# Four attention layers on one core: the last step of the row maxima goes from VectorE to GpSimd, with another table of slots and PSUM banks

## The chip, the core and the metric

One core of a Trainium2 chip runs the whole program. Its engines are TensorE (PE; its weight loads are shown apart as PEld), VectorE (DVE), ScalarE (ACT), GpSimd (POOL) and the DMA queues, issued here by SyncE (SP). Each engine takes its own instructions in order, and engines wait for one another by semaphores. The metric is the device time of one execution in microseconds (us); the median of the runs counts.

## The reference

Four attention blocks on one sequence of S = 2048 rows, D = 576, H = 32 heads of 18 columns, all in float32. Layers 0 and 2 (kind A) have keys and values for each head; layers 1 and 3 (kind B) share one key and one value head.

```python
x = x + A(layernorm(x));  x = x + B(layernorm(x));  x = x + A(layernorm(x));  x = x + B(layernorm(x))

def A(x, wqkv, wo):                        # B: the same with one k and one v for all heads
    q, k, v = split_heads(x @ wqkv)        # [H, S, 18]
    scores = einsum("hqd,hkd->hqk", q, k) * 18 ** -0.5
    p = softmax(scores, axis=-1)
    return merge_heads(einsum("hqk,hkd->hqd", p, v)) @ wo
```

## The kernel before

**Stages.** Each layer has a prologue (layer norm, transposition, projections to q, k and v through HBM), a main part (the attention), and an output projection that runs into the next layer's prologue. The main part works on pairs of heads `p` (16 pairs) and blocks `u` of 512 queries (4 a pair), so it has 64 windows `w = 4p + u` a layer and 256 in the program.

**One window.** The softmax needs the maximum of each query's scores before the exponentials, so every window does two things side by side: it takes the maxima of window `w + 2` (scores with queries on partitions, then a maximum along the row) and the exponentials of window `w` (scores again, now with keys on partitions and with the maximum subtracted inside the product), and multiplies the exponentials by the values. Heads `a = 0, 1` of the pair stand in the two halves of the array and their products run side by side.

**The table of slots.** `UNIT` writes the order of a window by hand. It has 32 slots; each slot is a pair of products, one for each head, and names what reads them: `e` an exponential (ACT), `m` a maximum over 512 keys (DVE, `reduce_max`), `d` a Relu of a score difference (ACT), `t` the combination of that difference with the second product (DVE, one custom instruction and a read of its accumulator). A pair `d`, `t` takes the maximum over two blocks of keys with one DVE instruction. `ee*` and `mm*` let one instruction read both banks. A number behind a slot says how many columns of probabilities-times-values (`oacc`, `pv_cols`) PE does there; 4096 a window. Slots between two numbers are called a group here: PE does the group's products into banks and then the columns.

**The table of banks.** `BANKS` names the two PSUM banks (of seven) that a slot's products go to. Before, it has four rows of 32 slots, used in turn by window. A product waits until the bank's last reader, on ACT or DVE, is done.

**The last step of the maxima.** The 32 partial maxima of a window (8 groups of 4) are columns of `mxd[w % 2]`. When the last is issued, `max_final` makes the negated maximum `neg` [128 x 8] of each group of four with one DVE reduction; GpSimd splits it into a rounded part and a rest (`hl`). Some slots later (`max_store`, `NM_AT = 3` steps) DVE transposes `hl` to `tr`; a DMA stores it, and another (`max_rows`) loads it into the rows of `big` that the exponentials of two windows later read.

**Other names.** `track_banks` wraps PE, ACT and DVE: it replaces the dependencies that come of the one big PSUM tile by waits on the readers of a bank alone (`met` adds what was made by instructions that the call's other operands overlap). `ptile` hands out halves of two-bank SBUF buffers from one list (`halves`), for staging in the prologue. All PE, ACT and DVE work is recorded at line 153, which is the wrapper's; GpSimd's work has its own lines (323 is `copy`).

Of the kernel before, what the change touches and what calls it, by code (L numbers as in the profile page):

```python
# [19 lines left out]
P = 128  # L20
# [44 lines left out]

UNIT = """ee* mt 256 ee* em te 384 md ee* mt 512 me em em 384 me em me 384 ee* me em 448 me mm ee 320
          md em 256 ee* dm mm 384 ee* em me 384 mm* ee em 384 me"""

BANKS = """01 63 45 26 01 36 45 20 13 62 45 03 16 24 01 53
# [6 lines left out]
           46 01 25 36 40 13 56 20 41 56 30 42 01 56 34 25"""  # L78
LAST = "ee* ee* 640 " + "ee* ee* 512 " * 6 + "ee* ee* 384"
LAG = 1152  # L80

# [78 lines left out]
def track_banks(tc, banks):  # L160

    nc = tc.nc
    readers, made = {}, {}

    def span(x):
        row = x.ap[0][0]
        c0 = x.offset % row
        return c0, c0 + sum((n - 1) * step for step, n in list(x.ap)[1:]) + 1

    def others(args):  # L170
        return [x for x in args if isinstance(x, bass.AP) and x.tensor.name != banks.tensor.name]

    def banks_in(args):
        got = set()
        for x in args:
            if isinstance(x, bass.AP) and x.tensor.name == banks.tensor.name:
                c0, c1 = span(x)
                got.update(range(c0 // 512, (c1 - 1) // 512 + 1))
        return got

    def met(args):
        keep = []
        for x in others(args):
            c0, c1 = span(x)
            keep += [i for d0, d1, i in made.get(x.tensor.name, []) if c0 < d1 and d0 < c1]
        return keep

    def free(i, engines, keep):
        for e in engines:
            tc.declare_no_dep(i.ins, group=e, keep=[x.ins for x in keep], reason="other banks")  # L190

    def order(i, earlier):
        for x in earlier:
            tc.add_manual_dep(i.ins, x.ins.name, mybir.DependencyInfo(mybir.DependencyClass.Sync,
                                                                     mybir.DependencyReason.ANTI), reason="one bank")

    def wrote(i, args, kw):
        for b in banks_in(args[:1]):
            last = [x for _, x in readers.pop(b, [])]
            free(i, ("act", "dve"), last + met(args[1:3]))  # L200
            order(i, last)

    def read(engine, other, i, args, kw):
        args = [*args, *kw.values()]
        got = banks_in(args)
        if got:
            beside = [x for b in sorted(got) for e, x in readers.get(b, []) if e == other]
            free(i, (other,), beside + met(args))
            order(i, beside)
            tc.add_to_no_dep_group(engine, i.ins)  # L210
            for x in others(args):
                made.setdefault(x.tensor.name, []).append((*span(x), i))
            for b in got:
                readers.setdefault(b, []).append((engine, i))

    return (Engine(nc.tensor, wrote), Engine(nc.scalar, functools.partial(read, "act", "dve")),
            Engine(nc.vector, functools.partial(read, "dve", "act")))


@with_exitstack  # L220
def tile_kernel(ctx: ExitStack, tc: tile.TileContext, A_x, A_wqkv, A_wo, B_x, B_wq, B_wk, B_wv, B_wo, out):
# [75 lines left out]
    def etile(name):  # L297
        return turn_of("e", name)

    halves = []  # L300

    def two(name):
        return pool.tile([P, 2, 512], F32, tag="p", bufs=8, name=name)

    def ptile(name, shape=(P, 512), dt=F32):
        if not halves:
            t = two(name)
            halves.extend([t[:, 0], t[:, 1]])
        t = halves.pop(0)
        if dt != F32:  # L310
            t = t.bitcast(dt)
        if len(shape) == 2:
            return t
        return t[:, :shape[1] * shape[2]].rearrange("p (a b) -> p a b", a=shape[1])
# [11 lines left out]
    def load_w(c, dsts, srcs, n, hi, lo, spare):  # L326


        raw = pool.tile([P, 640], F32, tag="xh", bufs=2, name="raw") if spare else ptile("raw")
# [24 lines left out]
    splits = []  # L354

    def finish_loads(n=99):
        while splits and n:
# [183 lines left out]
    for layer in range(4):  # L541
# [11 lines left out]
        def project(T, t, filler=False, half=None, terms=TERMS):  # L553
# [16 lines left out]
            if T < 2 and t in (range(4, 9) if is_a else (4,)):  # L570
                key_diff(T, t, ps, r0, r1)
            if filler:
                raw = ptile("evr")
                act.activation(raw[:n], ps[:n], AF.Copy)
                nc.gpsimd.tensor_tensor(ev[1][:n], raw[:n], ev_f[0][:n], op=OP.subtract)
            else:
                dve.tensor_tensor(ev[1][:n], ps[:n], ev_f[0][:n], op=OP.subtract)
            if not is_a and t == 4:
                vt = ptile("vt")
# [10 lines left out]
        def key_diff(T, t, ps, r0, r1):  # L590

            if T == 0:
                k0s[t] = ptile("k0")
                act.activation(k0s[t][r0:r1], ps[r0:r1], AF.Copy)
                return
            kd, lo, hi = k0s.pop(t), ptile("kl"), ptile("kh", dt=F32R)
# [289 lines left out]
            load_q(0, 512, S)  # L886

        def max_final(p, u):
            neg = pool.tile([P, 8], F32, name="neg")
            dve.tensor_reduce(neg, mxs.pop((p, u)).rearrange("p (b k) -> p b k", k=4), axis=AX.X, op=OP.max,  # L890
                                    negate=True)
            hl = nms[p, u] = hls[(4 * p + u) % 2]
            copy(nc.gpsimd, hl[:, 0:8], neg)
            nc.gpsimd.tensor_tensor(hl[:, 8:16], neg, hl.bitcast(F32)[:, 0:8], op=OP.subtract)
# [147 lines left out]
        kept.extend([etile("psm") for _ in range(weave["left"])])  # L1042
        fill[-1][0](*fill[-1][1])
        assert not weave["left"] and not kept
        side = xtile("side", (P, 9, 512), F32)
        late, n_r, n_p, sided = LAG, [0], [0], {}
        for w in range(4 * NPAIR):
# [67 lines left out]
```

## Time and profile before

| what | value |
|---|---|
| median of 3 runs (lowest, highest) | 5566.91 us (5565.56, 5570.06) |
| the profiled execution's own time | 5563.2 us |
| its span, first to last instruction | 5561.4 us |
| busy: PE, DVE, ACT, POOL | 5530.8, 5008.6, 4712.7, 1072.8 us |
| granted clock of TensorE | 0.999 |
| windows in which `neg` is made from `mxd` | 248 of 256 |

A row of the instruction groups reads: line, engine, operation, out<-in, shapes, count, busy us, mean ns of one. A row of the timeline reads: start us, us, engine, line, operation, names, shapes, how many merged, and in brackets the idle time before it and what ended it. DVE and ACT instructions overlap their neighbours at both ends, so what one costs is the distance from its start to the next one's start, which is less than its duration. A busy PE is not a PE at its peak, since the ends of products are modelled.

### The profile page before, as it was taken

The numbers are of one execution on the slowest core, as the hardware profiler recorded it, in microseconds if no ns is written. First come the engines' busy times: TensorE is split into PE (matmuls) and PEld (weight loads), VectorE is DVE, ScalarE is ACT, GpSimd is POOL, SyncE is SP. The second block draws the span as 40 slices with busy tenths as digits, with TensorE's granted clock in tenths as the row PEclk, the third lists the DMA queues.
The fourth block names the chain that finished last, engine by engine and source line by source line (L and its number), as shares of the span: only waits on it lengthen the run. The fifth ranks groups of instructions, "written<-read, shape, count | busy, mean of one in ns | idle before, by whom it ended". The sixth has DMA issues, their size and how long they took to land. (4 is left out here: it accounts for less than half of the span.)

```text
span 5561.4 us, 159140 instructions
## 1 busy us (share of the span) xinstructions
PE 5530.8 (99%) x63772; PEld 3174.9 (57%) x63772; DVE 5008.6 (90%) x9260; ACT 4712.7 (85%) x8020; POOL 1072.8 (19%) x1731
## 2 busy tenths in 40 slices
PE   9999999999999999999999999999999999999999
PEld 7655555555855555555686555555558555555556
DVE  5799999998699999999647999999977999999995
ACT  3599999999289999999625999999992999999995
POOL 3121111112121111112221211111122211111111
PEclk9999999999999999999999999999999999999999
DMA  7311111111421110101253211111114211110102
GB/s 235 114 48 39 40 38 41 37 38 32 129 64 25 24 25 21 25 21 25 62 198 96 51 39 37 40 37 41 34 39 133 54 24 25 24 25 21 25 14 81
DMA packets 295504, 295.03 MB, mean 53 GB/s; under 512 B 151133, under 2 KB 228189, under 8 KB 285041
## 3 DMA queue, kind: packets, MB, share of 16 engines
q1 hardware_dynamic: 294760, 284.85, 18.5%
q8 instruction: 499, 8.18, 0.6%
q14 instruction: 245, 2.00, 0.1%
HBM read 158.77 MB, written 121.95 MB: 50 GB/s over the span
## 5 line engine op out<-in xcount | busy, mean ns | idle before, releaser
L153 DVE TENSOR_REDUCE mxd<-banks 128x1 f32<-128x512 f32 (+1 forms) x6200 | 3995.4, 703 | 92.2 <-PE banks L153 20.4
L153 ACT ACTIVATE pt<-banks 128x512 f32<-128x512 f32 (+1 forms) x4408 | 2887.5, 716 | 136.2 <-PE banks L153 93.8
L153 PE MATMUL banks<-big 62*128 62x512 f32 (+1 forms) x15640 | 2818.4, 435 | 6.9 <-DVE mx L153 3.2
L153 PEld LDWEIGHTS banks<-big 62*128 62x128 f32 (+1 forms) x15640 | 1551.8, 185 | 1301.9 <-DVE mxd L153 499.4
L153 ACT ACTIVATE side<-banks 128x512 f32<-128x512 f32 (+1 forms) x2916 | 1864.7, 684 | 71.6 <-PE banks L153 53.2
L153 PE MATMUL oacc<-pt,vbuf 128*19 128x256 f32 (+3 forms) x21152 | 1287.9, 336 | 0.0
L153 PEld LDWEIGHTS oacc<-pt,vbuf 128*19 128x19 f32 x21152 | 460.4, 98 | 492.8 <-issue 330.8
L973 POOL TENSOR_TENSOR rl<-lt,mone 128x8 f32<-128x8 f32 x256 | 420.0, 1640 | 1634.5 <-DMA lt<-os 1611.2
L153 PE MATMUL oacc<-side,vbuf 128*19 128x128 f32 (+3 forms) x10400 | 684.3, 335 | 0.2 <-DVE ocv L153 0.2
L153 DVE CUSTOM_DVE_ANT_0 side<-banks,side 128x512 f32<-128x512 f32 x744 | 506.7, 681 | 0.0
L323 POOL TENSOR_SCALAR hl<-neg 128x8 fp32r<-128x8 f32 x256 | 51.7, 202 | 2144.2 <-DVE neg L153 2144.2
L153 PE MATMUL oacc<-pt,vy 128*19 128x128 f32 (+1 forms) x7520 | 436.0, 325 | 0.0
L153 PEld LDWEIGHTS oacc<-side,vbuf 128*19 128x19 f32 x10400 | 229.9, 98 | 238.9 <-issue 158.8
L153 PE MATMUL banks<-kd,big 54*128 54x512 f32 x744 | 344.2, 463 | 0.0
L153 ACT ACTIVATE ev<-banks 128x512 fp32r<-128x512 f32 (+3 forms) x107 | 63.6, 597 | 248.4 <-PE banks L153 144.8
L153 PEld LDWEIGHTS oacc<-pt,vy 128*19 128x19 f32 x7520 | 176.4, 98 | 156.0 <-issue 105.8
L153 PE MATMUL banks<-wsm,ot 128*128 128x288 f32 x1792 | 243.7, 296 | 2.1 <-issue 2.1
L153 PEld LDWEIGHTS banks<-wsm,ot 128*128 128x128 f32 x1792 | 238.4, 188 | 6.4 <-issue 5.2
L153 PE MATMUL oacc<-side,vy 128*19 128x128 f32 (+1 forms) x3680 | 232.8, 325 | 0.0
L153 DVE TENSOR_TENSOR ev<-banks,ev 128x512 fp32r<-128x512 f32 (+3 forms) x77 | 52.8, 690 | 183.6 <-ACT ev L153 144.4
L153 PE MATMUL banks<-xx,big 128*128 128x512 f32 (+1 forms) x784 | 198.4, 402 | 5.0 <-ACT evr L153 2.5
L153 PE MATMUL banks<-yx,big 128*128 128x512 f32 (+2 forms) x812 | 196.4, 395 | 5.1 <-DVE yx L153 3.3
(98 smaller groups left out, 2391.5 us busy)
## 6 DMA issues: line engine op xcount, KB each, us to landing
big<-qk_d SPq DMA_DIRECT2D x180, 432.0 KB
qk_d<-ev SPq DMA_DIRECT2D x73, 512.0 KB
qk_d<-ev SPq DMA_DIRECT2D x114, 256.0 KB
rb<-r_d SPq DMA_DIRECT2D x1024, 18.0 KB
o_d<-os SPq DMA_DIRECT2D x1024, 18.0 KB
lt<-os SPq DMA_DIRECT2D x1024, 1.0 KB
o<-o_d SPq DMA_DIRECT2D x62, 256.0 KB
big<-m_d SPq DMA_DIRECT2D x512, 4.0 KB
```

The lines of the kernel that those rows point to most:

```text
L153: i = f(*args, **kw)
L323: eng.tensor_scalar(dst, src, 1.0, 0.0, op0=OP.mult, op1=OP.add)
L973: nc.gpsimd.tensor_tensor(rl, lts.pop((p, u)), mone, op=OP.pow)
```

## The change

- `max_final` no longer uses DVE. Six GpSimd instructions stand for the one reduction: a maximum is written as the positive part of a difference plus the other value, first for columns 0, 1 against 2, 3 of each group (into the new tile `tree`), then for the two that are left. The split into `hl` follows on GpSimd as before.
- `UNIT` and `BANKS` are replaced. A window still has 32 slots, 26 `m` (two of them joined in one `mm*`), 3 `d`, 3 `t` and 32 `e`, 11 groups and 4096 columns; `ee*` stands 7 times where it stood 6 times. `BANKS` has one row of 32 slots for every window.
- `track_banks` compares operands by their exact runs of columns, where it took one span from the first to the last column, and keeps the last 64 instructions that made or read a tensor.
- `ptile` keeps a list of halves for each first letter of a name, and some names change so that they share one (`evr` becomes `raw`, `k0` becomes `first`, `vt` becomes `t`). The first weight load and the key staging of `t == 4` use `ocv`. The lists are emptied before the main part.

```diff
-UNIT = """ee* mt 256 ee* em te 384 md ee* mt 512 me em em 384 me em me 384 ee* me em 448 me mm ee 320
-          md em 256 ee* dm mm 384 ee* em me 384 mm* ee em 384 me"""
+UNIT = """me md em 320 ee* me et 384 em me me 448 em ee* mm 384 ee* dm mm 384 ee* tm ed 512 em mm* ee
+          256 me me 256 ee* mm me 320 em ee* et 448 me ee* mm 384"""
-BANKS = """01 63 45 26 01 36 45 20 13 62 45 03 16 24 01 53
...
+BANKS = """13 06 45 23 16 04 51 23 64 05 12 34 56 03 12 34
+           56 10 23 45 16 02 31 45 62 01 36 45 12 03 45 62"""
@@ track_banks
-    def span(x):
-        row = x.ap[0][0]
-        c0 = x.offset % row
-        return c0, c0 + sum((n - 1) * step for step, n in list(x.ap)[1:]) + 1
+    def runs(x):
+        row, *dims = [list(d) for d in x.ap]
+        at = [x.offset % row[0]]
+        for step, n in dims[:-1]:
+            at = [c + step * i for c in at for i in range(n)]
+        step, n = dims[-1]
+        return [(c, c + step * (n - 1) + 1) for c in at]
...
-                made.setdefault(x.tensor.name, []).append((*span(x), i))
+                made[x.tensor.name] = [*made.get(x.tensor.name, [])[-63:], (runs(x), i)]
@@ tile_kernel
+    tree = cst.tile([P, 8, 4], F32, name="tree")
...
-        if not halves:
+        left = halves.setdefault(name[0], [])
+        if not left:
             t = two(name)
-            halves.extend([t[:, 0], t[:, 1]])
-        t = halves.pop(0)
+            left.extend([t[:, 0], t[:, 1]])
+        t = left.pop(0)
...
-                k0s[t] = ptile("k0")
+                k0s[t] = ocv if t == 4 else ptile("first")
@@ max_final
+            mx = mxs.pop((p, u)).rearrange("p (b k) -> p b k", k=4)
+            above, left = tree[:, :, 0:2], tree[:, :, 2:4]
+            nc.gpsimd.tensor_tensor(above, mx[:, :, 0:2], mx[:, :, 2:4], op=OP.subtract)
+            nc.gpsimd.tensor_scalar(above, above, 0.0, None, op0=OP.max)
+            nc.gpsimd.tensor_tensor(left, above, mx[:, :, 2:4], op=OP.add)
             neg = pool.tile([P, 8], F32, name="neg")
-            dve.tensor_reduce(neg, mxs.pop((p, u)).rearrange("p (b k) -> p b k", k=4), axis=AX.X, op=OP.max,
-                                    negate=True)
+            nc.gpsimd.tensor_tensor(neg, left[:, :, 0], left[:, :, 1], op=OP.subtract)
+            nc.gpsimd.tensor_scalar(neg, neg, 0.0, -1.0, op0=OP.max, op1=OP.mult)
+            nc.gpsimd.tensor_tensor(neg, neg, left[:, :, 1], op=OP.subtract)
             hl = nms[p, u] = hls[(4 * p + u) % 2]
```

**What moves on DVE.** The rows below are DVE's queue from the end of one window's maxima to a little behind the transposition, in the main part of layer 0, before the change and after it. `ISA` is the custom instruction `t`, the `ISA` row behind it the read of its accumulator; `PE_49`, `DVE_49`, `Pool_49` and the like are the semaphores of the engines, `DMAHW` those of DMAs.

```order
L153 ISA side_1944,mxd0_100<-banks_86,side_1944 128x512 [waits PE_49,Activation_49]
L153 ISA mxd0_100 128x1
L153 TENSOR_REDUCE neg_11577<-mxd0_100 128x8 [waits DVE_49]
L153 TENSOR_REDUCE mxd1_101<-banks_86 128x1 [waits PE_49] x6
L153 STREAM_TRANSPOSE tr_11637<-hl0_104 128x32 [waits DMAHW6_49,Pool_49]
L153 TENSOR_REDUCE mxd1_101<-banks_86 128x1 [waits PE_49] x12
```

```order
L147 TENSOR_REDUCE mxd1_102<-banks_86 128x1 [waits PE_49]
L147 TENSOR_REDUCE mxd1_102<-banks_86 128x1 [waits DVE_49,PE_49]
L147 TENSOR_REDUCE mxd0_101<-banks_86 128x1 [waits DVE_49,PE_49] x4
L147 TENSOR_REDUCE mxd0_101<-banks_86 128x1 [waits PE_49]
L147 TENSOR_REDUCE mxd0_101<-banks_86 128x1 [waits DVE_49,PE_49] x2
L147 STREAM_TRANSPOSE tr_8069<-hl1_106 128x32 [waits DMAHW7_49,DVE_49,Pool_49]
```

The reduction to `neg` is gone from DVE, seven reductions stand ahead of the transposition where six stood, and many reductions now wait for DVE's own semaphore besides PE's. Such a wait is for the same column's earlier write: `mxd` has two tiles in turn, so that write was issued two windows before.

**What moves on POOL.** One window of GpSimd's queue in the same place, before and after. `os` are the sums of the value product, `rl` the reciprocals of the softmax's denominators.

```order
L323 TENSOR_SCALAR hl1_105<-neg_8388 128x8 [waits DVE_49]
L894 TENSOR_TENSOR hl1_105<-neg_8388,hl1_105 128x8 [waits Pool_49]
L323 TENSOR_SCALAR os1_98<-ocv_99 128x256 [waits DMAHW3_49,DMAHW2_49,DMAHW4_49,DMAHW1_49,Activation_49]
L987 TENSOR_TENSOR os0_97<-os0_97,rb_96 128x256 [waits DMAHW3_49,DMAHW4_49,DMAHW2_49,DMAHW1_49]
L973 TENSOR_TENSOR rl_8555<-lt_8452,mone_75 128x8 [waits DMAHW6_49,DMAHW7_49,DMAHW1_49,DMAHW0_49]
```

```order
L893 TENSOR_TENSOR tree_99<-mxd0_101 128x8x2 [waits DVE_49]
L894 TENSOR_SCALAR tree_99<-tree_99 128x8x2 [waits Pool_49]
L895 TENSOR_TENSOR tree_99<-tree_99,mxd0_101 128x8x2 [waits Pool_49]
L897 TENSOR_TENSOR neg_8747<-tree_99 128x8 [waits Pool_49]
L898 TENSOR_SCALAR neg_8747<-neg_8747 128x8 [waits Pool_49]
L899 TENSOR_TENSOR neg_8747<-neg_8747,tree_99 128x8 [waits Pool_49]
L319 TENSOR_SCALAR hl0_105<-neg_8747 128x8 [waits Pool_49]
L902 TENSOR_TENSOR hl0_105<-neg_8747,hl0_105 128x8 [waits Pool_49]
L319 TENSOR_SCALAR os0_97<-ocv_100 128x256 [waits DMAHW6_49,DMAHW5_49,DMAHW7_49,DMAHW4_49,Activation_49]
L995 TENSOR_TENSOR os1_98<-os1_98,rb_96 128x256 [waits DMAHW6_49,DMAHW7_49,DMAHW5_49,DMAHW4_49]
L981 TENSOR_TENSOR rl_8656<-lt_8570,mone_75 128x8 [waits DMAHW6_49,DMAHW7_49,DMAHW1_49,DMAHW0_49]
```

Six instructions more stand ahead of the copy to `os`, each waiting for the one before it; the order behind them is the same.

**What moves on PE.** PE's queue in one window, two groups with the columns between them, before and after (a row's bank product is one head's; `x4` on `oacc` is one piece of columns for four quarters of the array).

```order
L153 MATMUL banks<-big 128x512 [waits Activation_49]
L153 MATMUL banks<-kd,big 128x512 [waits DVE_49]
L153 MATMUL banks<-big 128x512 [waits Activation_49] x2
L153 MATMUL oacc<-side,vbuf 19x256 x4
L153 MATMUL banks<-big 128x512 [waits DVE_49]
L153 MATMUL banks<-big 128x512 [waits Activation_49]
L153 MATMUL banks<-kd,big 128x512
L153 MATMUL banks<-big 128x512 [waits Activation_49]
L153 MATMUL banks<-big 128x512 [waits DVE_49]
L153 MATMUL banks<-big 128x512 [waits Activation_49]
L153 MATMUL oacc<-pt,vbuf 19x256 x4
L153 MATMUL oacc<-pt,vbuf 19x128 x4
```

```order
L147 MATMUL banks<-big 128x512 [waits DVE_49]
L147 MATMUL banks<-big 128x512
L147 MATMUL banks<-kd,big 128x512 [waits Activation_49]
L147 MATMUL banks<-big 128x512 [waits DVE_49]
L147 MATMUL banks<-big 128x512 [waits Activation_49]
L147 MATMUL banks<-big 128x512
L147 MATMUL oacc<-side,vbuf 19x128 x4
L147 MATMUL oacc<-pt,vbuf 19x256 x4
L147 MATMUL banks<-big 128x512 [waits DVE_49]
L147 MATMUL banks<-big 128x512
```

The group of two slots (`md em 256`) that stood ahead of `ee* dm mm 384` is gone from that place, and `ee* dm mm 384` now follows a group of three; the window has as many products and columns as before, in another order and with other waits.

More of the change, by code (lines that the diff above doesn't have):

```diff
@@ L173, in banks_in @@
     def banks_in(args):
[L174 to L179, printed above, removed]
+        return {b for x in args if isinstance(x, bass.AP) and x.tensor.name == banks.tensor.name
+                for c0, c1 in runs(x) for b in range(c0 // 512, (c1 - 1) // 512 + 1)}
     def met(args):
@@ L183, in met @@
         for x in others(args):
-            c0, c1 = span(x)
-            keep += [i for d0, d1, i in made.get(x.tensor.name, []) if c0 < d1 and d0 < c1]
+            own = runs(x)
+            keep += [i for used, i in made.get(x.tensor.name, [])
+                     if any(c0 < d1 and d0 < c1 for c0, c1 in own for d0, d1 in used)]
         return keep
@@ L298, in etile @@
         return turn_of("e", name)
-    halves = []
+    halves = {}
     def two(name):
@@ L326, in load_w @@
     def load_w(c, dsts, srcs, n, hi, lo, spare):
-        raw = pool.tile([P, 640], F32, tag="xh", bufs=2, name="raw") if spare else ptile("raw")
+        if spare:
+            raw = pool.tile([P, 640], F32, tag="xh", bufs=2, name="raw")
+        elif not loaded[0]:
+            raw = ocv
+        else:
+            raw = ptile("raw")
+        loaded[0] += 1
         if sum(s_.shape[1] for s_, _ in srcs) < n:
@@ L352, in load_w @@
         splits.append(split)
-    splits = []
+    splits, loaded = [], [0]
     def finish_loads(n=99):
@@ L572, in project @@
             if filler:
[L573 removed]
+                raw = ptile("raw")
                 act.activation(raw[:n], ps[:n], AF.Copy)
@@ L1044, in tile_kernel @@
         assert not weave["left"] and not kept
+        halves.clear()
         side = xtile("side", (P, 9, 512), F32)
```

3 lines of the change are left out of this document (1 added, 2 removed), and 6 rows, old and new, of the table BANKS.

## The prediction

> **What bounds the kernel now.** I read the page's engine shares first, then the period of one window, then the timelines of DVE, PE and ACT inside one window. The period comes from the starts of `neg`, which is made once a window (first row: 16 of them, first and last start); the second row is the busy time of PE, PEld, DVE, ACT and POOL in that stretch.
>
> ```profile
> PE 5530.8 (99%) x63772; PEld 3174.9 (57%) x63772; DVE 5008.6 (90%) x9260; ACT 4712.7 (85%) x8020; POOL 1072.8 (19%) x1731
> L153 DVE TENSOR_REDUCE neg<-mxd x16: 185/186/189, 515.2 to 792.1; 128x8 f32<-128x32 f32 x16
> 515.20:792.10 276.90, 276.90 (x3484) 146.29 (x3482) 271.14 (x496) 265.16 (x451) 47.15 (x75) 1.00 0.16 39
> ```
>
> A window takes (792.1 - 515.2) / 15 = 18.46 us, and 248 such windows make 4578 us, 82% of the span. PE, DVE and ACT all look full there, so the busy shares decide nothing. What counts is how much work each engine has in a window when it never waits. For DVE that is read from starts:
>
> ```profile
> 699.95 0.19 DVE L153 TENSOR_REDUCE neg<-mxd 128x8 f32<-128x32 f32 x1
> 700.06 3.67 DVE L153 TENSOR_REDUCE mxd<-banks 128x1 f32<-128x512 f32 x6
> 703.64 0.20 DVE L153 STREAM_TRANSPOSE tr<-hl 128x32 f32<-128x32 f32 x1
> 703.77 10.59 DVE L153 TENSOR_REDUCE mxd<-banks 128x1 f32<-128x512 f32 x16
> 714.27 0.68 DVE L153 CUSTOM_DVE_ANT_0 side<-banks,side 128x512 f32<-128x512 f32 x1
> 714.88 0.08 DVE L153 DVE_READ_ACCUMULATOR2_ANT mxd<- 128x1 f32 x1
> ...
> 718.22 0.08 DVE L153 DVE_READ_ACCUMULATOR2_ANT mxd<- 128x1 f32 x1
> 718.34 0.19 DVE L153 TENSOR_REDUCE neg<-mxd 128x8 f32<-128x32 f32 x1
> 718.44 1.88 DVE L153 TENSOR_REDUCE mxd<-banks 128x1 f32<-128x512 f32 x3
> L153 DVE TENSOR_REDUCE mxd<-banks 128x2 f32<-128x1024 f32 x248 | 304.1, 1226 | 7.0 <-PE banks L153 0.3
> ```
>
> Six reductions start within 703.64 - 700.06 = 3.58 us, so one costs 0.597 us, 0.085 less than its duration. `neg` costs 718.44 - 718.34 = 0.10 us, `tr` 0.13, a `t` 0.61 and its accumulator read 0.12, the joined reduction 1.226 - 0.085 = 1.14. DVE's own work is 24 x 0.597 + 1.14 + 3 x 0.73 + 0.10 + 0.13 = 17.89 us; it waits 18.46 - 17.89 = 0.57 us a window. Most of that is inside the row of 16: it needs 15 x 0.597 + 1.14 = 10.10 us and takes 714.27 - 703.77 = 10.50.
>
> PE's rows show bank groups and columns in turn:
>
> ```profile
> 710.75 1.07 PE L153 MATMUL banks<-big 62*128 62x512 f32 x6
> 711.76 0.84 PE L153 MATMUL oacc<-pt,vy 128*19 128x256 f32 x16
> 712.53 1.18 PE L153 MATMUL banks<-big 62*128 62x512 f32 x6
> 713.65 0.41 PE L153 MATMUL oacc<-pt,vy 128*19 128x128 f32 x8
> ...
> 717.77 0.98 PE L153 MATMUL banks<-big 62*128 62x512 f32 x6
> 718.68 0.85 PE L153 MATMUL oacc<-pt,vbuf 128*19 128x256 f32 x16
> 719.46 1.07 PE L153 MATMUL banks<-big 62*128 62x512 f32 x6
> 720.46 0.41 PE L153 MATMUL oacc<-pt,vbuf 128*19 128x128 f32 x8
> ```
>
> A group of three slots that waits for nothing takes 718.68 - 717.77 = 0.91 us. Three groups of this window take longer: 1.01 (at 710.75), 1.12 (712.53) and 1.00 (719.46), together 0.40 us. So PE's own pace is about 18.46 - 0.40 = 18.06 us a window, slower than DVE's, and the whole period is PE's pace plus three short waits for banks. Who keeps those banks is told by the waits in the same stretch, and ACT's own work by its timeline:
>
> ```profile
> PEld banks L153 <- DVE mxd L153: 30.4, 91, 0.4
> PEld banks L153 <- ACT pt L153: 12.0, 44, 0.4
> PEld banks L153 <- ACT side L153: 8.8, 34, 0.4
> 699.64 0.43 ACT L153 ACTIVATE ocv<-oacc 128x256 f32<-128x256 f32 x1
> 709.70 1.02 ACT L153 ACTIVATE side<-banks 128x1024 f32<-128x1024 f32 x1 [0.23 <-PE banks L153]
> 710.62 2.06 ACT L153 ACTIVATE pt<-banks 128x512 f32<-128x512 f32 x4
> 712.53 1.17 ACT L153 ACTIVATE side<-banks 128x512 f32<-128x512 f32 x2
> ```
>
> The waits are for DVE (30.4 us) and for ACT (12.0 + 8.8 = 20.8 us), most of them PE's turn from columns to banks and not lost time. ACT's two-bank read costs 710.62 - 709.70 = 0.92 us, a single one (712.53 - 710.62) / 4 = 0.477, the copy of `oacc` at most its 0.43: 6 x 0.92 + 23 x 0.477 + 0.43 = 16.92 us. **PE at 18.06, DVE at 17.89 and ACT at 16.92 us are bound together in 18.46**; a gain is to be had from the 0.40 us that PE waits, and no more.
>
> **The change part by part.**
>
> *`neg` leaves DVE.* 248 x 0.10 = 25 us of DVE's time. On the path it is worth that if PE's waits for DVE come down in step, and 0 if those waits end on ACT; ends -25 and 0. I take -25, since the larger share of PE's waits is DVE's. Its wait for the accumulator read goes with it.
>
> *Six instructions more on POOL.* Their price is the distance between two that wait for one another:
>
> ```profile
> 515.51 0.20 POOL L323 TENSOR_SCALAR hl<-neg 128x8 fp32r<-128x8 f32 x1 [7.75 <-DVE neg L153]
> 515.79 0.20 POOL L894 TENSOR_TENSOR hl<-neg,hl 128x8 fp32r<-128x8 f32 x1
> 515.99 0.40 POOL L323 TENSOR_SCALAR os<-ocv 128x256 f32<-128x256 f32 x1
> 524.90 1.64 POOL L973 TENSOR_TENSOR rl<-lt,mone 128x8 f32<-128x8 f32 x1 [7.81 <-DMA lt<-os]
> 700.23 0.20 POOL L323 TENSOR_SCALAR hl<-neg 128x8 fp32r<-128x8 f32 x1 [8.93 <-DVE neg L153]
> 703.87 0.59 SPq L900 DMA_DIRECT2D m_d<-tr  x1
> 704.57 2.91 SPq L969 DMA_DIRECT2D lt<-os  x4
> ```
>
> That is 515.79 - 515.51 = 0.28 us, so the chain of eight takes 8 x 0.28 = 2.2 us; its first three work on 16 columns a partition, not 8, but even the copy of 256 columns takes only 0.20 us more than `hl`, so at most 3 x 0.20 = 0.6 us comes on top. The first starts about 700.23 - 699.95 - 0.19 = 0.09 us behind DVE's last maximum. `tr` stands seven reductions later, 7 x 0.597 = 4.2 us: it finds `hl` ready with about 1.9 us to spare, so DVE waits for nothing. Behind the chain POOL's copy to `os` comes about 1.7 us later (6 x 0.28); it ended near 701.1 in the second window, so now near 702.8 to 703, and the queue issues its DMA (`lt<-os`) only at 704.57, behind the one that waits for `tr`. The reciprocal behind it idles 7.81 us for that DMA. POOL idles 7.75 us ahead of the chain, so 1.7 us more is covered: cost 0; were the cover gone, `tr` would come 1.7 us late on DVE.
>
> [...]
>
> *Waits of DVE on itself.* The order shows about 15 a window. Each is for a write two windows old (37 us), done long before. Nearest row: `tr` has two waits already and starts at the same 0.597 us behind the reduction before it. Cost 0. If such a wait cost what the overlap is worth, 0.085 us, it would be 15 x 0.085 = 1.3 us a window; that is the other end, and a rival below.
>
> *`ee*` seven times.* Two single reads (0.954 us) become one of 0.92: 0.034 us x 248 = 8 us less on ACT. Ends -8 and 0 (ACT has 1.5 us free, but short of a bank at single places); I take -8, since PE's waits name ACT too.
>
> *Other slots and banks.* PE's products, columns and groups are the same in number (11 groups, one of two slots), so its own 18.06 us stay. What changes is where it waits: at best the 0.40 us go, 248 x 0.40 = 99 us; at worst a wait is added (below). By the reductions' prices, groups hold 1.20 to 1.92 us of DVE's work before and 1.20 to 1.79 after; every bank was and is reused at the earliest two slots later. Those are small differences. I take 0, with ends -99 + 33 = -66 (what is left beside the two terms above) and +104 (two places as long as the longest wait, 248 x 2 x 0.21).
>
> *Prologues: lists of halves, `ocv`, exact ranges.* Rows of a prologue stretch, of what waits for buffers there in the whole run, and of the one place where `tr` already waits for `hl`:
>
> ```profile
> 1440.00:1480.00 40.00, 39.90 (x233) 34.50 (x233) 27.38 (x65) 10.50 (x24) 7.44 (x16) 1.00 0.32 105
> ACT ev L153 <- DMA qk_d<-ev: 25.7, 10, 2.7
> DVE ev L153 <- DMA qk_d<-ev: 22.6, 9, 2.6
>   DVE tr L153: 1.1, 4
> ```
>
> PE is full there (39.90 of 40) while DVE and ACT are not; waits for a staging buffer, 25.7 and 22.6 us, lie beside PE's work. Where `tr` comes soon behind the maxima (4 times) the longer chain adds up to 4 x 1.7 = 7 us to DVE, beside 13 us that DVE has free in such a stretch. PE idles 5561.4 - 5530.8 = 31 us in the whole run, part of it before the first loads have landed; I take 0, with ends -10 and +10, a third of that.
>
> *Sum.* -25 - 8 + 0 + 0 + 0 = -33 us on the profiled execution's own 5563.2 us (span 5561.4): 5530 us. The median of the runs is 5566.9, 3.7 above that execution; against it the gain would be 0.7%. About 0.2%, 11 us, is what this measurement can tell from no change.
>
> **The rivals.**
>
> *PE's waits close.* DVE's and ACT's earlier releases, together with the other banks, take away most of the 0.40 us: 248 x 0.40 = 99, so 5464; half-way cases end near 5490. For it: DVE's own work falls to 17.79, 0.27 below PE's. Against it: DVE waits 0.57 us already and PE still finds banks taken, so spare time alone doesn't open them. Chance 0.15, for all below 5500.
>
> *No change.* PE's three waits end on ACT (the waits for `pt` and `side` are 20.8 us), and DVE only waits longer: 5563, within 11. For it: DVE isn't the slowest of the three now. Chance 0.14.
>
> *Slower: one bank more comes too late.* In the new table slot 13's maximum goes to bank 3, last read by slot 11's first maximum, with one reduction (0.597 us) behind it on DVE. PE can start it only when that read is over, and a product that finds nothing ahead of it takes half a microsecond:
>
> ```profile
> 724.60 0.50 PE L153 MATMUL banks<-big 62*128 62x512 f32 x1
> ```
>
> One reduction doesn't cover the end of the read (0.085 us) and that product (0.50 us) by much, 0.01 us without any hand-over. So DVE may run dry there, and PE behind it. A late bank costs what the longest of the three waits costs now, 1.12 - 0.91 = 0.21 us. It decides when it adds more than the 0.13 us that the two terms save: 248 x (0.21 - 0.13) = +20, so 5583; two such places give 248 x 0.29 = +72, 5635. Chance 0.17.
>
> *Slower: the waits cost DVE its overlap.* 248 x (1.3 - 0.10) is about +298, near 5860, if a wait holds an instruction until the one before it has ended. Against it stands the pace of the rows above. Chance 0.04. [...]
>
> **How the numbers follow.** The forecast, 5500 to 5552 (its own range), has 0.50. Faster is 0.50 + 0.15 = 0.65, within 0.2% 0.14, slower 0.17 + 0.04 = 0.21. The likeliest time is 5530. The range reaches down to 5455, past the floor of 5464 by the prologue's end of 10, and up to 5592, which takes in one late bank (5583) and leaves out two and the lost overlap.
>
> **What the profile after would show.** Right: no reduction to `neg` on DVE, reductions still 0.60 us apart, windows of about 18.33 us between transpositions (18.46 - 0.13), POOL's chain of eight in about 2.2 us, no row in which `tr` waits for `hl` in the main part, PE's long groups still there but shorter. Wrong: a period that is unchanged with PE still waiting for ACT; or gaps of DVE at the first reduction of a group behind slot 13; or reductions 0.68 us apart. What would make the forecast wrong above all is the table: three places of 0.1 to 0.2 us are the whole reserve, and the new one puts them where no row of before shows.

## The result, and the profile after

The changed kernel takes 5535.28 us (median of 6 runs, 5533.99 to 5536.69), the kernel before 5567.4 us (median of 6, 5565.56 to 5570.06). The ratio is 0.9943, with a 95% interval of 0.9933 to 0.9953: faster by 32 us. The profiled execution took 5534.68 us, 28.5 less than that of before. The prediction said 5530.

The engines' busy time on the page of the changed kernel (whose wrapper records PE, ACT and DVE work at line 147, and whose `copy` is line 319):

```profile
PE 5494.3 (99%) x63772; PEld 3242.2 (59%) x63772; DVE 4936.3 (89%) x9004; ACT 4709.4 (85%) x7780; POOL 1424.3 (26%) x3267
```

DVE has 256 instructions fewer, POOL 1536 more, and PE as many as before. The transpositions of the stretch that was used before (first and last start of 15), and the waits there:

```profile
L147 DVE STREAM_TRANSPOSE tr<-hl x15: 201/202/203, 532.4 to 789.2; 128x32 f32<-128x32 f32 x15
```

```profile
PEld banks L147 <- DVE mxd L147: 32.6, 90, 0.4
PEld banks L147 <- ACT pt L147: 11.6, 32, 0.4
...
DVE mxd L147 <- PE banks L147: 6.5, 33, 0.3
PEld banks L147 <- ACT side L147: 5.8, 16, 0.4
```

A window takes (789.2 - 532.4) / 14 = 18.34 us, where it took 18.46. PE's waits for DVE are no less than before (32.6 us against 30.4); those for ACT's `side` fell from 8.8 to 5.8. DVE now waits for PE for 6.5 us in the stretch; the row of the kernel before was

```profile
DVE mxd L153 <- PE banks L153: 1.2, 7, 0.2
```

So a part of the time that DVE was given went into waiting. DVE's timeline in one window, with the reductions and the transposition at the end:

```profile
715.84 0.20 DVE L147 STREAM_TRANSPOSE tr<-hl 128x32 f32<-128x32 f32 x1
...
717.38 5.41 DVE L147 TENSOR_REDUCE mxd<-banks 128x1 f32<-128x512 f32 x8 [0.16 <-PE banks L147]
...
728.66 5.58 DVE L147 TENSOR_REDUCE mxd<-banks 128x1 f32<-128x512 f32 x9 [0.22 <-PE banks L147]
734.16 0.20 DVE L147 STREAM_TRANSPOSE tr<-hl 128x32 f32<-128x32 f32 x1
```

POOL's chain, on its timeline in an earlier window (its transposition is the one at 532.4):

```profile
528.22 0.21 POOL L893 TENSOR_TENSOR tree<-mxd 128x16 f32<-128x16 f32 x1 [6.84 <-DVE mxd L147]
...
530.36 0.20 POOL L902 TENSOR_TENSOR hl<-neg,hl 128x8 fp32r<-128x8 f32 x1
530.56 0.40 POOL L319 TENSOR_SCALAR os<-ocv 128x256 f32<-128x256 f32 x1
```

The chain takes 530.56 - 528.22 = 2.34 us (2.2 were forecast) and is done 1.8 us ahead of the transposition (1.9). PE's timeline shows what is left of the long groups:

```profile
721.12 1.09 PE L147 MATMUL banks<-big 64*128 64x512 f32 x6
722.14 0.52 PE L147 MATMUL oacc<-side,vy 128*19 128x192 f32 x8
...
726.27 1.12 PE L147 MATMUL banks<-big 64*128 64x512 f32 x6
727.31 0.74 PE L147 MATMUL oacc<-pt,vy 128*19 128x64 f32 x16
...
728.09 0.96 PE L147 MATMUL banks<-big 64*128 64x512 f32 x6
728.99 0.52 PE L147 MATMUL oacc<-side,vy 128*19 128x192 f32 x8
```

A group lasts from its first row to the columns behind it: 1.02 us (`em ee* et`), 1.04 (`ee* me et`) and, in one that waits for nothing, 0.90. Over some 240 windows of the main parts the three long groups of before had means of 0.996 (`mm* ee em`), 1.109 (`me ee* mt`) and 0.998 (`me em me`), 0.39 above 3 x 0.905. Now there are two, 1.001 (`em ee* et`) and 1.052 (`ee* me et`), 0.24 above 2 x 0.905. These 0.15 us less, with some 0.03 more spread over other groups, are the 0.12 by which the mean window is shorter. The 60 windows of each layer between its first two and last two, 240 in all, take 4403.4 us instead of 4432.9, -29.5. That is the whole change of the span, and what lies around them cancels to within 1 us.

### The profile page after: what moved, and what is told of

Same layout as the page of the kernel before. It is cut to its first block, busy times and chain, and to the rows that moved or that the text cites. A ratio compares the mean times of both kernels' runs of the same rounds, so it can differ in the third digit from the quotient of the medians.

```text
span 5532.5 us, 163956 instructions
## 1 busy us (share of the span) xinstructions
PE 5494.3 (99%) x63772; PEld 3242.2 (59%) x63772; DVE 4936.3 (89%) x9004; ACT 4709.4 (85%) x7780; POOL 1424.3 (26%) x3267
## 4 chain that ended last, share of the span: by engine, by line
PE 96%; DVE 1%; ACT 1%; issue 0%; SPq 0%; DMA 0%; POOL 0%; ACTq 0%; DVEq 0%; POOLq 0%
PE banks L147 58%; PE oacc L147 38%; DVE mx L147 1%; ACT pt L147 0%; ACT side L147 0%; DMA qk_d<-ev 0%; DVE yx L147 0%; DVE xx L147 0%; DVE xh L147 0%; SPq L977 0%; ACT raw L147 0%; ACT ev L147 0%; DVE ev L147 0%; SPq L1000 0%; DVE st L147 0%
## 5 line engine op out<-in xcount | busy, mean ns | idle before, releaser
L147 DVE TENSOR_REDUCE mxd<-banks 128x1 f32<-128x512 f32 (+1 forms) x6200 | 3955.6, 705 | 143.5 <-PE banks L147 112.6
L147 ACT ACTIVATE pt<-banks 128x512 f32<-128x512 f32 (+1 forms) x4248 | 2927.9, 740 | 120.5 <-PE banks L147 83.3
L147 ACT ACTIVATE side<-banks 128x512 f32<-128x512 f32 (+1 forms) x2836 | 1907.2, 697 | 66.0 <-PE banks L147 65.6
L147 PE MATMUL oacc<-side,vbuf 128*19 128x256 f32 (+3 forms) x10064 | 676.9, 341 | 2.3 <-DVE ocv L147 2.3
L893 POOL TENSOR_TENSOR tree<-mxd 128x16 f32<-128x16 f32 x248 | 53.1, 214 | 1860.3 <-DVE mxd L147 1860.3
L147 PE MATMUL oacc<-pt,vy 128*19 128x256 f32 (+3 forms) x8176 | 444.1, 312 | 0.0
L147 ACT ACTIVATE ev<-banks 128x512 fp32r<-128x512 f32 (+1 forms) x112 | 66.9, 598 | 321.6 <-PE banks L147 245.3
L147 PE MATMUL banks<-kd,big 54*128 54x512 f32 x744 | 295.2, 397 | 0.0
L147 PE MATMUL oacc<-side,vy 128*19 128x256 f32 (+3 forms) x4016 | 240.7, 311 | 0.0
L147 DVE TENSOR_TENSOR ev<-banks,ev 128x512 fp32r<-128x512 f32 (+1 forms) x84 | 57.9, 690 | 171.6 <-ACT ev L147 156.3
```

The source lines that it names most:

```text
L147: i = f(*args, **kw)
L893: nc.gpsimd.tensor_tensor(above, mx[:, :, 0:2], mx[:, :, 2:4], op=OP.subtract)
```

## Which part did it

Three kernels take the change apart, on one chip beside 5564.9 us for the kernel before.

**`neg` on GpSimd alone** (the kernel before with the six instructions, old table):

```diff
@@ max_final of the kernel before
-            dve.tensor_reduce(neg, mxs.pop((p, u)).rearrange("p (b k) -> p b k", k=4), axis=AX.X, op=OP.max,
-                                    negate=True)
+            (the six nc.gpsimd instructions of the change)
```

> The kernel before with the last step of the maxima on GpSimd and nothing else changed (old slots and banks, old spans, one list of halves). Theory (DVE's 0.10 us a window is on the path whatever the table): the window falls from 18.47 to about 18.37 us, 248 x 0.10 = 25 us faster, ratio about 0.9955. Rival (the table makes the gain; PE's three late groups end on ACT or on DVE reads that neg does not delay): the window stays within 0.03 us of 18.47, ratio 0.9985 to 1.001, and DVE waits 0.1 us longer a window.

Measured: 5564.42 us, ratio 0.9998 (0.9989 to 1.0006). Nothing is gained, as the rival said. DVE's timeline behind a transposition:

```profile
704.90 0.20 DVE L153 STREAM_TRANSPOSE tr<-hl 128x32 f32<-128x32 f32 x1
705.02 1.25 DVE L153 TENSOR_REDUCE mxd<-banks 128x1 f32<-128x512 f32 x2
706.48 9.23 DVE L153 TENSOR_REDUCE mxd<-banks 128x1 f32<-128x512 f32 x14 [0.22 <-PE banks L153]
```

The third reduction waits for PE. From the second one's start to the third one's, the mean over the windows grew from 825 to 932 ns: the 0.10 us of `neg` is found again as a wait, and PE's long groups stay as they were (0.992, 1.113, 0.996).

The weight loads of the kernel before show what holds its long groups, here `mm* ee em` (at 710.75) and `me ee* mt` (at 712.53):

```profile
710.75 0.30 PEld L153 LDWEIGHTS banks<-big 62*128 62x128 f32 x4 [0.42 <-DVE mxd L153]
711.26 0.25 PEld L153 LDWEIGHTS banks<-big 64*128 64x128 f32 x2 [0.21 <-ACT pt L153]
...
712.53 0.53 PEld L153 LDWEIGHTS banks<-big 62*128 62x128 f32 x5 [0.21 <-issue]
713.22 0.18 PEld L153 LDWEIGHTS banks<-big 62*128 62x128 f32 x1 [0.16 <-ACT side L153]
```

In this table a group's length follows its last weight load (means over the 240 windows). In the groups of three slots that are not long the sixth load starts at most 0.48 us into the group, and the group takes 0.90 to 0.91 us. In `mm* ee em`, `me ee* mt` and `me em me` it starts at 0.57, 0.68 and 0.57, and these groups are longer by as much. The wait that makes it late, at the fifth load in the first of them and at the sixth in the others, names ACT in 240, 240 and 218 of the windows, and DVE in none. So the long groups end on ACT's reads, and a DVE that is 0.1 us earlier doesn't shorten them.

**The new table alone** (the kernel before with the new `UNIT` and `BANKS`, `neg` on DVE):

```diff
-UNIT = """ee* mt 256 ...        (old UNIT and BANKS)
+UNIT = """me md em 320 ...      (new UNIT and BANKS)
```

> The kernel before with the new slots and banks alone; neg stays on DVE. Theory that neg carries the gain: within 0.1% of before or slower, window 18.43 or more. Rival that the table carries it: the whole 0.15 us a window, 18.33, ratio about 0.9945. If both are needed (the new table leaves DVE the shorter waits that only a DVE without neg can use), between: 18.40 to 18.45, ratio 0.997 to 0.999.

Measured: 5589.95 us, ratio 1.0044 (1.0031 to 1.0057): slower by 25 us. Of the 11 groups ten are within 10 ns of those of the changed kernel; one, `ee* dm mm`, has a mean of 1.116 us instead of 0.912. These 0.204 us x 248 are 51 us. It is the place that the prediction named: slot 13's maximum goes into bank 3, which slot 11's reduction read last. The weight loads of that group, here:

```profile
721.86 0.19 PEld L147 LDWEIGHTS banks<-big 64*128 64x128 f32 x2 [0.21 <-DVE mxd L147]
721.97 0.19 PEld L147 LDWEIGHTS banks<-kd,big 54*128 54x128 f32 x1
722.32 0.29 PEld L147 LDWEIGHTS banks<-big 62*128 62x128 f32 x3 [0.17 <-DVE mxd L147]
722.97 0.14 PEld L147 LDWEIGHTS oacc<-pt,vbuf 128*19 128x19 f32 x8 [0.35 <-issue]
```

and in the changed kernel:

```profile
731.55 0.19 PEld L147 LDWEIGHTS banks<-big 64*128 64x128 f32 x2 [0.21 <-issue]
731.66 0.19 PEld L147 LDWEIGHTS banks<-kd,big 54*128 54x128 f32 x1
731.80 0.43 PEld L147 LDWEIGHTS banks<-big 62*128 62x128 f32 x3
732.47 0.14 PEld L147 LDWEIGHTS oacc<-side,vbuf 128*19 128x19 f32 x8 [0.24 <-issue]
```

The fourth load comes 722.32 - 721.86 = 0.46 us into the group instead of 731.80 - 731.55 = 0.25, and the columns start 1.11 us into it instead of 0.92. Why DVE is 0.2 us late though `neg` costs 0.10, its timeline tells:

```profile
718.97 1.29 DVE L147 TENSOR_REDUCE mxd<-banks 128x1 f32<-128x512 f32 x2 [0.24 <-PE banks L147]
720.29 0.19 DVE L147 TENSOR_REDUCE neg<-mxd 128x8 f32<-128x32 f32 x1
720.39 3.75 DVE L147 TENSOR_REDUCE mxd<-banks 128x1 f32<-128x512 f32 x6
```

Two reductions need 2 x 0.597 = 1.19 us from start to start, but `neg` starts 1.32 us behind the first. It reads the column that the second one writes and waits for its end (718.97 + 1.29 = 720.26; `neg` starts at 720.29). In the old table it stood behind an accumulator read, 0.12 us after it, where the next reduction without `neg` stands 0.09 after. So `neg` costs (means over the windows) 0.117 + 0.103 = 0.22 us of DVE in the new table, and 0.13 in the old one.

**Both, without the exact ranges and the lists of halves:**

```diff
-UNIT = """ee* mt 256 ...        (old UNIT and BANKS)
+UNIT = """me md em 320 ...      (new UNIT and BANKS)
@@ max_final of the kernel before
-            dve.tensor_reduce(neg, ...)
+            (the six nc.gpsimd instructions of the change)
```

> Both of these, without the exact ranges and without the sorted lists of halves. If those two cost and bring nothing: the time of the whole change within 0.1%, ratio 0.9935 to 0.9953. If they matter, the difference shows between the layers, not in the window, which should be 18.33 us either way.

Measured: 5537.72 us, ratio 0.995 (0.9937 to 0.9962), the whole change within the uncertainty; its 240 windows take 4403.4 us, the same to 0.1. The ratios are 0.0007 apart, some 4 us, which the intervals don't tell from nothing. If the ranges and the halves bring anything, it is of that size and lies outside these windows.

The parts do not add: -0.5 and +25 alone, -27 together. Without its one late bank the new table would be worth about 25 - 51 = -26 us, which is nearly the -27 of both.

## Is it DVE's time or the instruction's place?

The kernels of this section and the next ones were timed beside the kernel before, not beside the changed kernel, so a few us between one of them and the changed kernel say nothing.

**A reduction of `neg`'s size put back into the changed kernel**, whose result nobody uses:

```diff
+    pad = cst.tile([P, 8], F32, name="pad")
@@ max_final, behind the six GpSimd instructions
+            dve.tensor_reduce(pad, mx, axis=AX.X, op=OP.max, negate=True)
```

> The changed kernel with a reduction of neg's size put back on DVE where neg stood, reading mxd into a tile that nothing reads; GpSimd still makes neg, so only DVE's 0.10 us comes back (its waits on itself go, since this reduction waits once for all). Theory from the second run (0.10 us of DVE ahead of slot 13 makes bank 3 late, and a late bank costs PE 0.20 us): the group 'ee* dm mm' grows from 0.91 to about 1.11 us, the window from 18.33 to 18.54, 50 us slower than the changed kernel, ratio to before near 1.004. Rival (the second run was slow because neg and what hangs on it came from DVE, or by the waits): nearly the changed kernel's time, ratio 0.994 to 0.997.

Measured: 5591.12 us, ratio 1.0048 (1.0035 to 1.006); `ee* dm mm` is 1.118 us. DVE's time at this place is enough for a loss of 56 us (0.206 us x 248 = 51 of it in this group), with nobody waiting for the result. The same time at another place of DVE's queue was not tried. **Two of them:**

```diff
+            for i in range(2):
+                dve.tensor_reduce(pad[:, 8 * i:8 * i + 8], mx, axis=AX.X, op=OP.max, negate=True)
```

> The changed kernel with two reductions of neg's size put on DVE in a row, 0.20 us a window (one of them made the window 0.205 us longer). Theory (a step: once the bank of slot 13 is late, PE pays for the late weight load and product, and behind that delay counts one for one): window about 18.53 + 0.10 = 18.64, 76 us slower than the changed kernel, ratio to before near 1.009. Rival (delay counts twice): 18.74, 102 us slower, ratio near 1.013. Rival (the step has room: DVE's waits for PE take up the second 0.10): 18.54, ratio near 1.005.

Measured: 5608.44 us, ratio 1.0076 (1.0064 to 1.0089); the group is 1.211 us. The timeline of DVE with two:

```profile
719.85 1.29 DVE L147 TENSOR_REDUCE mxd<-banks 128x1 f32<-128x512 f32 x2 [0.24 <-PE banks L147]
721.17 0.28 DVE L147 TENSOR_REDUCE pad<-mxd 128x8 f32<-128x32 f32 x2
721.37 4.35 DVE L147 TENSOR_REDUCE mxd<-banks 128x1 f32<-128x512 f32 x7
```

The first costs PE 0.206 us, the second 0.093. When these runs were planned I took that for a step, paid once a product loses its early weight load. DVE's own means are a plainer reading: the first delays DVE by 0.117 (the wait for the column) + 0.103 = 0.22 us, the second, which waits for no fresh column, by 0.093. For these 0.31 us in sum PE's group grew by 0.299. I made no run with a pad that reads an older column, so the reading rests on these means.

**ACT's time: four `ee*` written as `ee`**, two reads of one bank instead of one of two:

```diff
-... em ee* mm 384 ee* dm mm 384 ee* tm ed 512 ... em ee* et 448 ...
+... em ee mm 384 ee dm mm 384 ee tm ed 512 ... em ee et 448 ...
```

> The changed kernel with four of the seven two-bank exponentials of a window as two single ones each: 4 x 0.034 = 0.14 us more on ACT, same banks, slots and columns. Theory of the prediction's second term (ACT's time counts one for one): window 18.47, 34 us slower than the changed kernel, ratio to before near 1.000. Rival (ACT has 1.5 us of room in a window and singles free a bank sooner than a joined read): window within 0.03 us of 18.33 or shorter, ratio 0.993 to 0.996.

Measured: 5567.45 us, ratio 1.0004 (0.9995 to 1.0013) to the kernel before, so 32 us lost against the changed kernel. By the prediction's price, 4 x 0.034 = 0.14 us more on ACT x 248 = 34; the window's median grew by 0.13, from 18.33 to 18.46. So it counts nearly one for one. It shows in three groups: `me me` 0.705 to 0.743, `me ee* mm` 0.908 to 0.941, `ee* dm mm` 0.912 to 0.968. At the places tested, then, neither ACT nor DVE has time to spare in this table, though ACT is busy for only 85% of the span.

## What costs nothing, and how far the cover goes

**One buffer for `tr`.** With it 3356 of DVE's waits on itself vanish (in the trace 2782 DVE instructions wait for DVE's own semaphore without it, and 392 with it):

```diff
-            tr = pool.tile([P, 32], F32, name="tr")
+            tr = pool.tile([P, 32], F32, bufs=1, name="tr")
```

> The changed kernel with one buffer for tr where it had two. The transposition then waits for its own last one, which covers every older write of mxd, and some 14 waits of DVE on itself in a window fall away (3356 in the program); the work is the same. Theory of the prediction (such a wait costs nothing): within 0.1% of the changed kernel, ratio to before 0.9940 to 0.9960, reductions 0.598 us apart in both. Rival (each costs 5 to 10 ns of DVE): 0.07 to 0.14 us a window less on DVE; with the late banks that is up to 25 us faster, ratio near 0.990.

Measured: 5535.51 us, ratio 0.9947 (0.9933 to 0.9961), as with the waits. By the interval of 0.14%, 8 us, a wait that is already met costs at most some 2 ns here.

**Twelve more GpSimd additions of zeros in the chain:**

```diff
@@ max_final, ahead of the split into hl
+            for _ in range(12):
+                nc.gpsimd.tensor_tensor(neg, neg, pad, op=OP.add)
```

> The changed kernel with twelve more GpSimd additions in the chain to hl (they add a tile of zeros, so the result stays): 12 x 0.29 = 3.5 us more, where the trace of the changed kernel shows 1.8 us between the end of hl and the transposition. Theory (the longer chain of the change is covered by 1.8 us, and no more): the transposition comes 1.7 us late and DVE stands still behind it, window 18.33 + 1.3 to 1.7, ratio to before 1.05 to 1.07, and the trace shows the transposition waiting for hl. Rival (the place of the transposition does not matter, since DVE has spare time): window within 0.1 us of 18.33.

Measured: 5980.25 us, ratio 1.0746 (1.0731 to 1.076). POOL's timeline (the twelve are merged), and `tr`'s waits in the whole run (us, times):

```profile
543.62 0.20 POOL L901 TENSOR_TENSOR neg<-neg,tree 128x8 f32<-128x8 f32 x1
543.90 3.27 POOL L903 TENSOR_TENSOR neg<-neg,pad 128x8 f32<-128x8 f32 x12
547.25 0.20 POOL L321 TENSOR_SCALAR hl<-neg 128x8 fp32r<-128x8 f32 x1
```

```profile
  POOL hl L906: 392.5, 254
```

The chain is 547.25 - 543.90 = 3.35 us longer; less the 1.8 of cover, 1.55 should be left, and DVE waits 392.5 / 254 = 1.55. The window's median is 19.89 us, 1.57 more than 18.33. That makes 388 of the 445 us; most of the rest is in some 25 windows of 21 us and more, which I did not trace and which take the ratio past the 1.07 that was expected. So the 1.86 us that the change added to GpSimd's chain (2.34, where its two instructions before took 515.99 - 515.51 = 0.48) left 1.8 us of cover, and in this run what went past that counted in full. No run lies between the two.

## Attempts on the two groups that are left

The four kernels below move columns or slots to give the bank of a long group more time. Columns of `oacc` per window are the same. e9 moves the banks of four slots besides the two that change places.

```diff
 e4:  me md em 384 ee* me et 384 em me me 384 em ee* mm     (were 320, 384, 448)
 e7:  me md em 384 ee* me et 320 em me me 448 em ee* mm     (were 320, 384, 448)
 e8:  ee* mm me 384 em ee* et 384 me ee* mm                 (were 320, 448)
 e9:  me em md 320 ...  with slots 0 to 15 of BANKS as 13 45 06 23 15 04 61 23 54 06 12 34 56 03 12 34
```

> The changed kernel with 64 columns moved between two groups of the table: 'me md em' gets 384 columns, not 320, and 'em me me' 384, not 448. The group 'ee* me et' between them is the longest of the new window, 1.05 us against 0.91, since its last product waits for a bank that ACT reads. Theory (that product is late only because PE comes 0.11 us too early): the group falls to about 0.95 us and the window from 18.33 to about 18.25, 20 us faster than the changed kernel, ratio to before near 0.991. Rival (ACT and PE are bound in a circle, and the wait moves to another group): the window stays within 0.03 us of 18.33, ratio 0.994 to 0.995.

> The changed kernel with 64 columns moved the other way round the long group: 'me md em' 384 (was 320) and 'ee* me et' 320 (was 384), so that PE comes 0.11 us later to 'ee* me et' and to all else when it did. Theory (a group is long only if a bank is late, and 'em me me' behind it has room): the group falls from 1.05 to 0.95 us and nothing else grows, window 18.23, 25 us faster than the changed kernel, ratio near 0.990. Rival (as in the run before with 448 to 384: the wait moves): the group falls and another grows by 0.1 to 0.2 us, ratio 0.994 to 0.999.

> The same at the second long group of the changed kernel: 'ee* mm me' gets 384 columns (was 320) and 'em ee* et' 384 (was 448). Theory: 'em ee* et' falls from 1.00 to 0.91 us, window 18.24, ratio near 0.990. Rival: the wait moves to 'me ee* mm' behind it, ratio 0.994 to 0.999.

> The changed kernel with two slots of the table exchanged ('me em md' for 'me md em', and banks to match: ACT's exponential of the second slot comes one Relu, 0.48 us, earlier). In the long group 'ee* me et' the last product waits for the bank of just that exponential. Theory (a group is long only because one bank's reader is late, and an order in which that reader comes earlier pays, where moved columns did not): that group falls from 1.05 to 0.91-0.95 us, nothing else grows, window 18.20 to 18.25, 20 to 30 us faster than the changed kernel, ratio to before 0.989 to 0.991. Rival (three engines in a circle: what PE gains there it loses at the next group): window within 0.05 us of 18.33, or longer, ratio 0.994 to 0.999.

Measured (group means in us over the main parts, worked out from PE's timeline as above):

| kernel | us | ratio to before | `me md em` | `ee* me et` | `em me me` | `em ee* mm` | `em ee* et` | `me ee* mm` |
|---|---|---|---|---|---|---|---|---|
| changed | 5535.28 | 0.9943 (0.9933 to 0.9953) | 0.904 | 1.052 | 0.900 | 0.906 | 1.001 | 0.908 |
| e4 | 5556.35 | 0.9987 (0.9978 to 0.9996) | 0.904 | 0.943 | 0.899 | 1.122 | 0.998 | 0.909 |
| e7 | 5560.02 | 0.9989 (0.9981 to 0.9998) | 0.902 | 0.943 | 0.949 | 1.071 | 0.997 | 0.909 |
| e8 | 5555.67 | 0.9982 (0.9973 to 0.9991) | 0.906 | 1.050 | 0.900 | 0.907 | 0.907 | 1.081 |
| e9 | 5633.2 | 1.0121 (1.0107 to 1.0135) | 1.123 | 1.225 | 0.902 | 0.902 | 1.003 | 0.908 |

The theory behind them, that a long group is short of columns ahead of it, fell each time. The group that got them went down (1.052 to 0.943, 1.001 to 0.907), and a group one or two places behind went up by more (0.906 to 1.122, 0.908 to 1.081). e7 and e8 came out as their rivals said. e4's rival, that the window stays within 0.03 us of 18.33, missed too: its median is 18.43. e9 is worse than both of its theories; the weight loads of its two long groups name one engine each:

```profile
701.98 0.30 PEld L147 LDWEIGHTS banks<-big 64*128 64x128 f32 x3 [0.27 <-ACT pt L147]
...
704.10 0.19 PEld L147 LDWEIGHTS banks<-big 64*128 64x128 f32 x2 [0.41 <-DVE mxd L147]
```

In the changed kernel the late load of `em ee* et` waits 0.27 us for ACT. In `ee* me et` the fifth load waits 0.10 us for DVE and the sixth 0.02 for ACT, where the first of these expectations named ACT alone. Whether the 0.24 us that are left can be had by another table stays open. No kernel beat the changed one.

## Why the prediction was right, and where it was not

- **The total and the window: right.** 5530 against 5535.28 us, 18.33 against 18.34 us.
- **The split of it: wrong.** The step that failed is "`neg` leaves DVE: I take -25", with the table at 0 (and -8 for its `ee*`), as terms to be added. Measured: `neg` alone -0.5, the table alone +25, together -27. The gain is the new table's, which has one long group less; `neg`'s move pays for that table's late bank, by 0.204 us x 248 = 51 us. My reason for -25, that most of PE's waits name DVE, was no measure: the row also counts PE's turns from columns to banks, which groups that are not long have too, while the late loads of the three long groups wait for ACT; and the same row stands at 32.6 us after the change. The two mistakes nearly cancel, so the right total is luck and no proof of its working.
- **"Slower: one bank more comes too late": right in place and price** (0.204 us measured for 0.21; slot 13), wrong in its condition. Whether that bank is late hangs on whether `neg` still runs on DVE, which is the other half of the same change; I should have costed the two together. That the price agrees is luck too: 0.21 was read from a wait of the old table that names ACT, and the 0.204 come from the 0.22 us that `neg` takes of DVE.
- **"PE's three waits end on ACT", no change: right for the move of `neg` alone.** The late loads of all three wait for ACT, and DVE only waited longer, as that rival said.
- **ACT's -8 us** were not tested against the old table. On the new one ACT's time counts nearly one for one, which bears out the price there.
- **POOL's chain, DVE's waits on itself, the prologues: right.** `tr` waited for `hl` 4.8 us in the whole run, 6 times, all in the first or last windows of a layer (up to 7 were allowed for). DVE's reductions kept their pace beside the chain: the nine among which it runs (730.03 to 732.37 on POOL) take 734.16 - 728.66 = 5.50 us, 0.11 of it a wait for PE, so 0.60 each; in the kernel before the six at 700.06 took 0.597 each, with `hl` on POOL at 700.23.
- **"Cost 0" for what stands behind the chain on POOL: wrong in two windows of 240,** near the ends of layers 0 and 2, of 20.07 and 19.29 us instead of 18.33. There POOL also prepares the next layer's weights. The timelines of POOL, SP and PE in the first of them:

```profile
1263.77 0.20 POOL L902 TENSOR_TENSOR hl<-neg,hl 128x8 fp32r<-128x8 f32 x1
1263.91 0.31 POOL L333 MEMSET raw<- 128x256 f32 x1
1264.19 0.41 POOL L319 TENSOR_SCALAR os<-ocv 128x256 f32<-128x256 f32 x1
```

```profile
1264.25 0.53 SPq L339 DMA_DIRECT2D raw<-in_B_wq_dram  x1
...
1268.29 0.60 SPq L908 DMA_DIRECT2D m_d<-tr  x1
...
1274.61 0.56 SPq L912 DMA_DIRECT2D big<-m_d  x2
```

```profile
SPq L339 <- POOL os L319: 4.6, 1, 4.6
PE banks L147 <- DMA big<-m_d: 1.3, 1, 1.3
```

  The last two rows are waits (us in total, times, longest) between 1258 and 1278 for SP and 1262 and 1287 for PE. SP's six weight loads, the first of them at 1264.25, wait 4.6 us for POOL, which clears `raw` only behind its chain (until 1263.91 + 0.31 = 1264.22). The store of `tr`, made at 1265.77, stands behind the six and is issued at 1268.29, the maxima's rows (`big<-m_d`) come late, and PE waits 1.3 us for them. (SPq rows are DMA issues.) SP in the kernel before, at the same loads:

```profile
1270.21 0.53 SPq L337 DMA_DIRECT2D raw<-in_B_wq_dram  x1
...
1275.80 0.60 SPq L900 DMA_DIRECT2D m_d<-tr  x1
```

  There `raw` was cleared at 1269.26, ahead of POOL's shorter chain; the loads start 5.4 us ahead of `tr` (1275.57), and the store follows it by 0.23 us. Part of the 1.3 us is something else: the issue of four `o_d<-os` ahead of `big<-m_d` takes 2.98 us in this window and 1.51 in the kernel before, and no run shows why. The two windows cost 2.7 us together. In the second SP's first weight load waits 4.5 us for POOL in the same way, and PE waits 0.5 us for the rows. Neither the new table alone nor `neg` on GpSimd alone has a window above 18.9 us, so here too it takes both.

## What to carry to other kernels

When several engines are bound together, the value of time taken off one of them isn't its sum: one reduction's 0.13 us were worth nothing under one table of banks, and its 0.22 us were worth 51 us under another. Ask of each removed instruction which buffer's release stood behind it, and cost a schedule and the engine's load together, not as two terms. A count of waits doesn't say which of them make the period longer; the late weight loads in the groups that are too long do (0.57 to 0.68 us into the group instead of at most 0.48 in the kernel before). A chain moved to an idle engine was free here within the distance to its first reader (1.86 us more of chain, 1.8 us still left), and the work queued behind it there, with the queues that wait for that work, needs the same look.

## What the runs showed of the hardware beyond what was expected

- In the runs with `neg` or a pad on DVE under the new table, a small DVE reduction that reads a column just written costs its own 0.103 us and another 0.117, since it starts only when the reduction before it has ended (720.29 behind 720.26 with `neg`, 721.17 behind 721.14 with two pads); behind another that reads the same columns it costs 0.093.
- A weight load that waits for a bank delays what stands behind it in its group: in the new table alone, 0.21 us late at the fourth load of `ee* dm mm`, 0.19 to 0.20 at the columns. An earlier wait can be free: in the kernel before, groups whose fifth load waited 0.16 us, until 0.46 us into the group, still took 0.90 to 0.91 us.
